# Three-stage kernel (causal attention, two expert layers): fixed places for early weight steps, a changed drain, and activations split by product

## The chip, the core and the metric

One core of one Trainium2 chip runs the whole program. The metric is the device time of one execution in microseconds, as the median of several runs. A profiled execution adds a trace: what each engine did and when, what ended its idle time, and the clock that TensorE was granted.

## The reference

Causal attention over 2 x 12 heads, 448 positions, 64 wide; then two feed-forward layers over the 896 rows of 768 columns, all in float32 accuracy (the weights come as 64-bit floats):

```python
scores = np.where(mask, -1e9, scale * q @ k.T)
attn = softmax(scores);  x = concat_heads(attn @ v)           # 896 x 768
h = x @ w_in                                                   # 768 x 2048
g = np.where(h >= 1, h, np.where(h <= -1, 0, (h + 1)**2 / 4))
x = g @ w_out                                                  # 2048 x 768
xn = x / rms(x) * rms_g
y = (silu(xn @ w_gate) * (xn @ w_val)) @ w_out2                # 768 x 1536, 1536 x 768
```

## The kernel before, in words

**Arithmetic.** A matrix operand is kept as two parts, a rounded high part and the rest, and a product of two such operands is three matmuls. `product` (L614) runs the three steps of 128 of half the inner size, so nine matmuls of 128x128 by 128x448. The w_in layer forms the output of a pair of column blocks for both batches with seven such products instead of eight (1 to 7, lines 723 to 770), out of sums and differences of blocks of the weights and of x. For the first four pairs products 1 and 2 are done early, as `head_in` and `tail_in` (L642, L646), so that five remain.

**Weights.** Each 128x768 block arrives by DMA into one of three stages (`w_load`, L141), always the next one in a fixed list `items`, and the load of a block waits until the block three places before it has left its stage (`w_next`, L149). The 64-bit words become float32 in steps: `w_scale` (GpSimd, L167, for the first NEARLY = 6 blocks, else ScalarE, L169), `w_low` (GpSimd, L177), `w_sign` (VectorE, L183, only where GpSimd scaled), `w_high` (VectorE, L195). Then the block is split (`parts`, L201: a cast on ScalarE, a subtraction on GpSimd), or, for a pair, first summed (`pair_steps` L416, `early_steps` L470: low, gate_high, val_high, sums_a, sums_b, hi, lo) and then split. A step is a small function; `steps` holds them in order, `ends` says where each block is finished, `w_run(n)` issues the next n up to a cap, `w_need(n)` issues all up to a block.

**Order.** Nothing is scheduled by a planner: each engine runs its instructions in the order in which the Python code issues them, so an instruction that waits holds all behind it on its engine. SP issues every DMA in the same way.

**Attention.** Twelve pairs of heads, three units each (L654). Per unit TensorE does scores, transposes of the exponentials and, once per pair, the spread of the factors (`spread`, L331) and the product with v (`pv`, L341); VectorE does the maxima (L277), ScalarE the exponentials (L285). One weight step is issued at the end of each unit from the second to the 35th (L701): first pairs 0 and 1 of the weights, then four plain blocks (the "gates") for the heads. When a pair's x is there, `xscale`, `xsplit` and `xmix` (L365 to L398) make the differences that the products need: T1 to T4, B11, B21, B22, each as high and low part.

**Drain.** Units 36 to 38 finish the last pair of heads. Heads and tails 0, 1, 2, 3 run there, two products to a unit, the product with v of the last pair between head 2 and tail 2 (L693 to L695); then its x is scaled, split and mixed.

**Layer with w_in.** For f = 0 to 7 a list `run` names the products in order (L792 to L799; pair f-1 still has 3 and 4 to do). After each product (L800):

```python
for p, g, n, late in run:
    IN[p][0](g)      # nine matmuls
    w_run(n)         # weight steps
    settle()         # clip of the product before
    IN[p][1](g)      # copy or sum, then relu and square
    w_run(late)
```

The activation is relu on ScalarE (L635), square on ScalarE (L637) or GpSimd (L639), and a clip on VectorE (L632) that `settle` issues later. Product 1 is copied out of its bank by ScalarE (L727) before product 6 adds into it; products 2, 4 and 5 are summed with earlier ones by VectorE (L718).

**w_out.** Sixteen blocks, three steps each, in a skewed order (L573): first step of block i, second of block i-1, third of block i-2. `out1` (L842) multiplies 18 matmuls per block. The second layer (from L961) follows the same plan as the first.

Of the kernel before, what the change touches and what calls it, by code (L numbers as in the profile page):

```python
# [41 lines left out]
def kernel(  # L42
# [14 lines left out]
    nc = tc.nc  # L57
# [16 lines left out]
    NEARLY = 6  # L74
# [290 lines left out]
    def xscale(g):  # L365
        b, p = divmod(g, NP)
        nc.vector.tensor_tensor(out=rb if b else X0[p], in0=xbank.pop(g)[:, :S], in1=rb, op=ALU.mult)

    def xsplit(g):
# [7 lines left out]
        else:  # L377
# [3 lines left out]
            if g == NG - 1:  # L381
                act_split(T2, k, t, nc.vector)
            else:
                pool_split(T2, k, t)
# [85 lines left out]
    def early_steps(n, f):  # L470
        bl = block(f)

# [12 lines left out]
        def gate_high():  # L485
            w_sign(n)
            w_high(n)
            w_low(n + 1)

        def val_high():  # L490
            w_sign(n + 1)
            w_high(n + 1)

        def sums_a():
            g, v, s12, s34 = halves(value(n)), halves(value(n + 1)), rest(n), rest(n + 1)
            tt(s12[:, 0], v[:, 0], v[:, 1], ALU.add)
            tt(s34[:, 0], g[:, 0], v[:, 0], ALU.subtract)

        def sums_b():
            g, s12, s34 = halves(value(n)), rest(n), rest(n + 1)  # L500
            tt(s12[:, 1], s12[:, 0], g[:, 0], ALU.subtract)
            tt(s34[:, 1], g[:, 1], s12[:, 1], ALU.subtract)
# [5 lines left out]
        def split_a():  # L508
            split(0, rest(n))
            w_next(n)  # L510

        def split_b():
            split(2, rest(n + 1))
# [5 lines left out]
        return [], [low, gate_high, val_high, sums_a, sums_b, split_a, split_b, split_c]  # L519
# [53 lines left out]
    def skewed(ws):  # L573
        for i in range(len(ws) + 2):
            for j in range(3):
# [5 lines left out]
    for w in work[:NW]:  # L581
        steps.extend(w)
        ends.append(len(steps))
    skewed(work[NW:NG2])
# [44 lines left out]
    def settle():  # L629
        while pending:  # L630
            out, u, x = pending.pop(0)
            nc.vector.scalar_tensor_tensor(out=out, in0=u, scalar=1.0, in1=x, op0=ALU.min, op1=ALU.max)  # L632

    def moe_act(out, u, x, eng=nc.scalar):
        nc.scalar.activation(u, x, ACTF.Relu, bias=half, scale=0.5)  # L635
        if eng is nc.scalar:
# [3 lines left out]
        pending.append((out, u, x))  # L640

    def head_in(f):  # L642
        product(bank(f), gop(f, 0), B11)
# [582 lines left out]
```

## Time and profile before

| | |
|---|---|
| median of 3 runs | 652.76 us (651.67 to 654.35) |
| the profiled execution, own time | 656.71 us |
| its span in the trace | 654.6 us |
| granted clock of TensorE, mean | 0.953 |
| busy: TensorE, VectorE, ScalarE, GpSimd | 597.6, 396.1, 349.5, 333.2 us |
| moved by DMA | 71.35 MB |

Busy time of TensorE counts matmuls at either clock level, so it is not time at full speed. An engine with time to spare can still hold up another one, if its instructions come in the wrong order; that is read from waits and timelines, not from busy shares.

### The profile page before, as it was taken

How to read it: one execution, taken by the hardware profiler on the slowest of the kernel's cores; microseconds unless marked ns; L12 is line 12 of the kernel's file. 1: busy time of each engine (PE TensorE's matmuls, PEld its weight loads, DVE VectorE, ACT ScalarE, POOL GpSimd, SP SyncE). 2: the span in 40 equal slices, each digit the busy share in tenths (PEclk: the TensorE clock that was granted, in tenths of full speed). 3: DMA queues.
4: the chain of work that ended last, by engine and by line, in shares of the span. 5: the costliest groups of instructions: out<-in, count | busy, mean ns of one | idle time of the engine just before them, and what ended most of it. 6: DMA issues, size and time to landing. Idle time of an engine off the chain costs nothing.

```text
span 654.6 us, 8698 instructions
## 1 busy us (share of the span) xinstructions
PE 597.6 (91%) x3164; PEld 508.7 (78%) x3164; DVE 396.1 (61%) x666; ACT 349.5 (53%) x698; POOL 333.2 (51%) x262
## 2 busy tenths in 40 slices
PE   6889999859959886589999999989999999999997
PEld 3556666748848785479889999979899999999996
DVE  4877888344664665347856684976565664896110
ACT  3767887435663555255476337755555555654211
POOL 3375656331675443349985543455555544894000
PEclk9897999878998888699999999998999999999999
DMA  8153533002332221245515320133353243551102
GB/s 285 44 182 119 183 105 126 1 1 97 96 105 88 97 96 48 103 164 208 201 49 193 102 91 8 42 117 124 105 173 109 98 132 114 189 192 47 39 0 86
DMA packets 17851, 71.35 MB, mean 109 GB/s; under 512 B 2128, under 2 KB 6736, under 8 KB 17808
## 3 DMA queue, kind: packets, MB, share of 16 engines
q1 hardware_dynamic: 17808, 70.79, 32.1%
q8 instruction: 25, 0.41, 0.2%
q14 instruction: 18, 0.15, 0.1%
HBM read 68.03 MB, written 2.75 MB: 108 GB/s over the span
## 4 chain that ended last, share of the span: by engine, by line
PE 71%; POOL 8%; ACT 7%; issue 5%; DVE 4%; DMA 4%; SPq 1%; POOLq 0%; DVEq 0%; ACTq 0%
PE ps L617 28%; PE ps L848 16%; PE ps L1160 14%; PE ps L270 4%; PE ps L301 4%; PE ps L349 4%; DMA af<-in_w_out 3%; POOL ar L203 2%; PE ps L335 2%; POOL af L177 1%; POOL af L639 1%; DVE af L355 1%; POOL ar L466 1%; ACT af L635 1%; ACT af L169 1%
## 5 line engine op out<-in xcount | busy, mean ns | idle before, releaser
L617 PE MATMUL ps<-ar 128*128 128x448 f32 x1260 | 277.9, 382 | 38.3 <-ACT af L727 14.5
L617 PEld LDWEIGHTS ps<-ar 128*128 128x128 f32 x1260 | 245.7, 197 | 68.4 <-ACT af L727 16.0
L203 POOL TENSOR_TENSOR ar<-af,ar 128x768 fp32r<-128x768 f32 (+1 forms) x56 | 101.2, 1809 | 97.9 <-ACT ar L202 85.8
L848 PE MATMUL ps<-ar 128*128 128x448 f32 x576 | 121.7, 372 | 2.5 <-POOL ar L203 1.8
L848 PEld LDWEIGHTS ps<-ar 128*128 128x128 f32 x576 | 109.0, 191 | 14.5 <-POOL ar L203 4.1
L177 POOL TENSOR_SCALAR af<-af 128x768 int32<-128x768 uint8 x76 | 83.4, 1097 | 23.2 <-DMA af<-in_w_out 17.3
L195 DVE SCALAR_TENSOR_TENSOR af<-af 128x768 int32<-128x768 int32 (+1 forms) x78 | 77.1, 992 | 24.1 <-POOL af L177 22.4
L1160 PE MATMUL ps<-ar 128*128 128x448 f32 x432 | 88.9, 367 | 0.0
L1160 PEld LDWEIGHTS ps<-ar 128*128 128x128 f32 x432 | 81.0, 188 | 7.7 <-DVE ar L1107 0.3
L169 ACT ACTIVATE af<-af 128x768 f32<-128x768 f32 x70 | 63.1, 909 | 44.0 <-DMA af<-in_w_out 44.0
L820 DVE TENSOR_TENSOR ar<-af,ar 128x448 fp32r<-128x448 f32 x32 | 46.5, 1471 | 23.6 <-ACT ar L819 23.6
L285 ACT ACTIVATE af<-ps,nm 112x336 f32<-112x336 f32 (+2 forms) x96 | 47.1, 504 | 22.9 <-DVE nm L277 22.8
L270 PE MATMUL ps<-af 64*112 64x448 f32 (+3 forms) x192 | 40.8, 476 | 10.5 <-DVE af L248 5.0
L202 ACT CAST ar<-af 128x768 fp32r<-128x768 f32 (+1 forms) x56 | 40.9, 731 | 17.5 <-DVE af L195 12.3
L632 DVE SCALAR_TENSOR_TENSOR af<-af,ps 128x448 f32<-128x448 f32 x24 | 14.9, 621 | 57.2 <-ACT af L637 40.2
L1107 DVE TENSOR_TENSOR ar<-af,ar 128x448 fp32r<-128x448 f32 x24 | 29.2, 1228 | 32.9 <-ACT ar L1106 32.8
L277 DVE CUSTOM_DVE_ANT_0 ps<-ps,af 112x336 f32<-112x336 f32 (+2 forms) x96 | 41.8, 469 | 8.4 <-PE ps L270 7.1
L466 POOL TENSOR_TENSOR ar<-af,ar 128x768 fp32r<-128x768 f32 x18 | 33.6, 1868 | 20.2 <-ACT ar L462 20.2
L270 PEld LDWEIGHTS ps<-af 64*112 64x112 f32 x192 | 18.7, 188 | 21.8 <-ACT af L285 6.2
L301 PE MATMUL ps<-ident,af 112*112 112x112 f32 x240 | 32.6, 278 | 2.0 <-ACT af L319 2.0
L635 ACT ACTIVATE af<-ps,half 128x448 f32<-128x448 f32 x24 | 15.2, 632 | 36.1 <-DVE ps L718 19.3
L941 POOL TENSOR_TENSOR ar<-af,ar 128x448 fp32r<-128x448 f32 x15 | 18.0, 1216 | 30.6 <-ACT ar L940 17.1
(101 smaller groups left out, 644.4 us busy)
## 6 DMA issues: line engine op xcount, KB each, us to landing
af<-in_w_out SPq DMA_DIRECT2D x28, 768.0 KB, 4.3
af<-in_w_in SPq DMA_DIRECT2D x20, 768.0 KB, 4.4
af<-in_w_gate SPq DMA_DIRECT2D x16, 768.0 KB, 4.4
af<-in_w_val SPq DMA_DIRECT2D x12, 768.0 KB, 4.3
af<-in_kT SPq DMA_DIRECT2D x12, 224.0 KB, 4.1
af<-in_qT SPq DMA_DIRECT2D x12, 224.0 KB, 4.3
af<-in_v SPq DMA_DIRECT2D x12, 224.0 KB, 2.8
out_T<-af SPq DMA_DIRECT2D x12, 224.0 KB, 1.9
```

The lines of the kernel that those rows point to most:

```text
L169: nc.scalar.activation(c, c, ACTF.Prelu, scale=2.0 ** -112, alpha=-2.0 ** 32)
L177: nc.gpsimd.tensor_scalar(out=words(n, 0, I32), in0=b, scalar1=1.0 / 32, scalar2=-31.0 / 64, op0=ALU.mult, op1=ALU.add)
L195: nc.vector.scalar_tensor_tensor(out=out.bitcast(I32), in0=words(n, 1, I32)[:, c], scalar=3, in1=words(n, 0, I32)[:, c], op0=ALU.logical_s ...
L203: nc.gpsimd.tensor_tensor(out=lo, in0=src, in1=b32(hi), op=ALU.subtract)
L270: nc.tensor.matmul(bs[j][:C, o:o + (c + 1) * C], lhsT=q[r, c * C:(c + 1) * C], rhs=k[r, :(c + 1) * C], start=True, stop=True, skip_group_c ...
L277: nc.vector.tensor_tensor_reduce(out=t, in0=t, in1=mask[:C, S - (c + 1) * C:], scale=-1.0, scalar=3e38, op0=ALU.add, op1=ALU.min, accum_ou ...
L285: nc.scalar.activation(Pn[:C, j, poff[c]:poff[c] + w], sbank[n][j][:C, o:o + w], ACTF.Exp, bias=nm[:C, j, c:c + 1], scale=-1.0, accum_out= ...
L301: nc.tensor.transpose(bs[j][:C, o:o + C], Pn[:C, j, poff[c] + kc * C:poff[c] + (kc + 1) * C], ident[:C, :C])
L617: nc.tensor.matmul(b[:, :S], lhsT=w(a, k), rhs=x[:, c, k], start=first and k == 0 and i == 0, stop=(k == HK - 1 and i == 2), skip_group_ch ...
L820: nc.vector.tensor_tensor(out=t[:, 1], in0=G[h][:, kk], in1=b32(t[:, 0]), op=ALU.subtract)
L848: nc.tensor.matmul(ybs[dm][:, :S], lhsT=w[:, a, dm * P:(dm + 1) * P], rhs=t[:, c], start=(n == 0 and i == 0), stop=(n == NM - 1 and i == 2))
L1160: nc.tensor.matmul(obs[dm][:, :S], lhsT=w[:, a, dm * P:(dm + 1) * P], rhs=t[:, c], start=(kk == 0 and i == 0), stop=(kk == NF - 1 and i == 2))
```

## The change

1. **Fixed table.** The gates come first in `items`, then the pairs. The steps of the gates and of pairs 0 and 1 are no longer in `steps`; a table `EARLY` names after which unit each of 37 steps is issued. NEARLY is 3. The steps of pair 0 and 1 are cut finer (eleven instead of eight).
2. **Second pair in the drain.** The last nine steps of pair 1 are placed at units 36 to 38. Its raw blocks and sums go to buffers that the attention has left by then.
3. **Product with v earlier.** Unit 36 runs only head 1, unit 37 the product with v and tail 1, unit 38 head 2, tail 2, head 3, tail 3.
4. **Last x in PSUM.** For the last pair of heads `xlast` takes the place of `xsplit` and `xmix`: x and the differences stay in PSUM banks, ScalarE casts, VectorE subtracts, in four pieces between the heads and tails.
5. **Activation split by product.** A sum or copy is issued right behind its product, then what `tick` finds due (relu and square at once, the clip one product later), then the weight steps. Some orders of products change (f = 1, f = 7).
6. **w_out steps.** The skewed order of the sixteen blocks runs back: third step of block i-2, second of i-1, first of i. The cap in f = 7 is one block lower.

The diff, cut (the finer cut of `early_steps`, names only changed, is left out):

```diff
-    NEARLY = 6
+    NEARLY = 3
...
     def xscale(g):
         b, p = divmod(g, NP)
-        nc.vector.tensor_tensor(out=rb if b else X0[p], in0=xbank.pop(g)[:, :S], in1=rb, op=ALU.mult)
+        x = xbank[g][:, :S] if g == NG - 1 else rb if b else X0[p]
+        nc.vector.tensor_tensor(out=x, in0=xbank[g][:, :S], in1=rb, op=ALU.mult)
...
+    def xlast():
+        g, k, p = NG - 1, HK - 1, NP - 1
+        x, t, x3, x4 = xbank[g][:, :S], bank(5)[:, :S], bank(6)[:, :S], bank(4)[:, :S]
+        sub(t, x, b32(T1[:, 0, k]))
+        sub(t, t, b32(T1[:, 1, k]))
+        yield
+        nc.scalar.copy(T2[:, 0, k], t)
+        sub(x3, t, X0[k])
+        sub(T2[:, 1, k], t, b32(T2[:, 0, k]))
+        yield
+        nc.scalar.copy(T3[:, 0, k], x3)
+        sub(x4, X0[p], t)
+        sub(T3[:, 1, k], x3, b32(T3[:, 0, k]))
+        yield
+        act_split(T4, k, x4, nc.vector)
+        act_split(B22, k, x, nc.vector)
+        yield
...
-        return [], [low, gate_high, val_high, sums_a, sums_b, split_a, split_b, split_c]
+        return [], [low, gate_high, val_low, val_high, sum_1, sum_3, sum_2, sum_4, split_a, split_b, split_c]
...
-    for f in range(2):
-        pair(f, True)
     for f in range(NA):
-        plain(w_in[PAIRS[f][0]], gslot(f), True)
-    for f in range(2, NPR):
+        plain(w_in[PAIRS[f][0]], gslot(f))
+    for f in range(NPR):
         pair(f, True)
...
-    def skewed(ws):
+    def skewed(ws, back=False):
         for i in range(len(ws) + 2):
-            for j in range(3):
+            for j in (2, 1, 0) if back else range(3):
...
-    skewed(work[NW:NG2])
+    skewed(work[NW:NG2], True)
...
+    EARLY = {(0, 2): ((0, 0), (0, 1), (1, 0)), (1, 2): ((0, 2),), (2, 0): ((0, 3),), (2, 2): ((1, 1),),
+             (3, 2): ((1, 2), (2, 0)), (4, 0): ((1, 3),), (4, 2): ((2, 1),), (5, 2): ((2, 2), (3, 0)),
+             (6, 0): ((2, 3),), (6, 2): ((3, 2), (4, 0)), (7, 0): ((3, 3),), (7, 2): ((4, 1), (4, 2)),
+             (8, 2): ((4, 3),), (9, 0): ((4, 4),), (9, 2): ((4, 5), (4, 6), (5, 0)), (10, 0): ((4, 7),),
+             (10, 2): ((4, 8),), (11, 0): ((4, 9),), (11, 1): ((4, 10),), (11, 2): ((5, 1),), (12, 0): ((5, 2),),
+             (12, 1): ((5, 3),), (12, 3): ((5, 4), (5, 5), (5, 6), (5, 7)), (12, 4): ((5, 8), (5, 9), (5, 10))}
...
             if g == NG:
-                head_in(2)
                 pv(g - 1)
-                tail_in(2)
+                tail_in(1)
         elif g == NG:
             xscale(g - 1)
-            xsplit(g - 1)
-            xmix(g - 1)
-        if 0 < n < NN - 1:
-            w_run(1)
-        if n in (NN - 1, NN, NN + 2):
-            f = n - NN + 1
-            w_need(4 + f + 1)
-            head_in(f)
-            tail_in(f)
+            mixing = xlast()
+            next(mixing)
+            head_in(2, lambda: next(mixing))
+            next(mixing)
+            tail_in(2)
+            settle()
+            next(mixing)
+            early(g, 3)
+            head_in(3)
+            tail_in(3)
+            early(g, 4)
+        early(g, u)
+        if n == NN - 1:
+            head_in(0)
+            tail_in(0)
+        elif n == NN:
+            head_in(1)
         settle()
...
         def in5(f):
-            x = gm(1, f, 1)
+            x, u = gm(1, f, 1), gm(1, f, 0)
             plus(x, yb[f], x)
             if 0 < f < NA - 1:
                 preload_in(f + 1)
-            moe_act(x, gm(1, f, 0), x, nc.gpsimd)
+            later(1, lambda: relu(u, x))
+            later(1, lambda: square(u, nc.gpsimd))
+            later(2, lambda: clip(x, u, x))
...
             if f == 0:
...
+                in6(0)
+                preload_in(1)
+                w_cap[0] = NA + 6
                 w_run(2)
-                in6(0)
-                settle()
-                preload_in(1)
...
-            w_cap[0] = 4 + NA + 2 * f if f < NPR - 1 else NW + 4
-            if f == 1:
-                run = [(6, 1, 2, 0), (3, 0, 1, 0), (7, 1, 0, 1), (4, 0, 1, 0), (5, 1, 0, 0)]
-            elif f < NA:
-                run = [(4, f - 1, 1, 0), (6, f, 1, 0), (3, f - 1, 2, 0), (7, f, 1, 1), (5, f, 1, 0)]
+            if f < NA:
+                run = [(4, f - 1, 1), (6, f, 1), (3, f - 1, 2), (7, f, 1), (5, f, 2)]
             elif f < NPR - 1:
-                run = [(p, f - (p in (3, 4)), 1, 0) for p in ((4, 1) if f == NA else (1, 4)) + (6, 3, 7, 5, 2)]
+                run = [(p, f - (p in (3, 4)), 1) for p in ((4, 1) if f == NA else (1, 4)) + (6, 3, 7, 5, 2)]
             else:
-                run = [(p, f - (p in (3, 4)), 2, 0) for p in (4, 3, 1, 6, 7, 2, 5)]
-                run[0] = (4, f - 1, 0, 0)
-            for p, g, n, late in run:
+                run = [(p, f - (p in (3, 4)), 1 + (p == 3)) for p in (4, 3, 1, 6, 7, 5, 2)]
+            for p, g, n in run:
                 IN[p][0](g)
+                IN[p][1](g)
+                tick()
                 w_run(n)
-                settle()
-                IN[p][1](g)
-                w_run(late)
```

The cap of the loop is now set ahead of it, to `NA + 2 * f + 4` for f < 7 and `NW + 3` for f = 7. Products 2, 3 and 4 are split as product 5 is; for 3 the relu follows at once. In the table (g, u) is the unit, the pair behind it a block (0 to 3 the gates, 4 and 5 the pairs) and one of its steps.

## Rows read from the trace of the kernel before

**Rows 1.** The page's head.

```profile
span 654.6 us, 8698 instructions
```

**Rows 2.** Busy time by stretch: PE, PEld, DVE, ACT, POOL, then granted clock.

```profile
0.00:64.00 64.00, 53.44 (x368) 33.28 (x368) 43.78 (x133) 39.62 (x124) 32.15 (x38) 0.89 0.47 159
...
115.00:148.60 33.60, 23.30 (x120) 18.80 (x121) 12.14 (x20) 12.70 (x26) 11.71 (x13) 0.85 0.00 1
148.60:275.00 126.40, 101.33 (x432) 88.70 (x433) 68.77 (x100) 64.72 (x104) 62.07 (x49) 0.88 0.27 89
```

**Rows 3.** The chain of waits in order of time: start, us, what.

```profile
19.32 0.92 PE ps L335 x16
...
62.47 0.92 PE ps L335 x16
...
70.32 0.92 PE ps L335 x16
...
255.64 4.18 DMA af<-in_w_out
...
459.19 103.05 PE ps L617 x504
```

**Rows 4.** VectorE's timeline: start, us, engine, line, tiles, idle before.

```profile
15.67 0.63 DVE L277 CUSTOM_DVE_ANT_0 ps<-ps,af 112x448 f32<-112x448 f32 x1
...
45.68 0.96 DVE L195 SCALAR_TENSOR_TENSOR af<-af 128x768 int32<-128x768 int32 x1 [0.79 <-POOL af L177]
...
126.62 0.20 DVE L328 RECIPROCAL rs<-rs 112x8 f32<-112x8 f32 x1
...
136.46 0.62 DVE L367 TENSOR_TENSOR af<-ps,af 128x448 f32<-128x448 f32 x1
...
156.33 0.62 DVE L718 TENSOR_TENSOR af<-ps,af 128x448 f32<-128x448 f32 x1 [5.98 <-PE ps L617]
...
208.50 2.24 DVE L632 SCALAR_TENSOR_TENSOR af<-af 128x448 f32<-128x448 f32 x1 [0.89 <-POOL af L639]
...
210.67 0.62 DVE L718 TENSOR_TENSOR ps<-ps,af 128x448 f32<-128x448 f32 x1
```

**Rows 5.** ScalarE's timeline.

```profile
211.38 0.63 ACT L635 ACTIVATE af<-ps,half 128x448 f32<-128x448 f32 x1 [3.92 <-DVE ps L718]
...
213.32 0.50 ACT L727 COPY af<-ps 128x448 f32<-128x448 f32 x1
```

**Rows 6.** TensorE's timeline.

```profile
130.47 2.11 PE L349 MATMUL ps<-af 112*64 112x336 f32 x20
...
143.07 3.64 PE L617 MATMUL ps<-ar 128*128 128x448 f32 x9 [6.65 <-ACT af L644]
...
148.62 21.65 PE L617 MATMUL ps<-ar 128*128 128x448 f32 x95 [1.92 <-ACT ps L721]
...
213.88 14.59 PE L617 MATMUL ps<-ar 128*128 128x448 f32 x63 [2.28 <-ACT af L727]
...
230.80 16.44 PE L617 MATMUL ps<-ar 128*128 128x448 f32 x72 [2.32 <-ACT af L727]
...
275.03 15.54 PE L848 MATMUL ps<-ar 128*128 128x448 f32 x72
...
293.74 53.68 PE L848 MATMUL ps<-ar 128*128 128x448 f32 x250 [1.80 <-POOL ar L203]
```

**Rows 7.** The page's costliest groups: count, busy us, mean ns, idle before.

```profile
L169 ACT ACTIVATE af<-af 128x768 f32<-128x768 f32 x70 | 63.1, 909 | 44.0 <-DMA af<-in_w_out 44.0
...
L466 POOL TENSOR_TENSOR ar<-af,ar 128x768 fp32r<-128x768 f32 x18 | 33.6, 1868 | 20.2 <-ACT ar L462 20.2
...
L462 ACT CAST ar<-af 128x768 fp32r<-128x768 f32 x18 | 15.1, 839 | 0.0
```

**Rows 8.** GpSimd's timeline in the w_out stage.

```profile
297.72 1.15 POOL L177 TENSOR_SCALAR af<-af 128x768 int32<-128x768 uint8 x1
...
301.66 1.15 POOL L177 TENSOR_SCALAR af<-af 128x768 int32<-128x768 uint8 x1
```

More of the change, by code (lines that the diff above doesn't have):

```diff
@@ L508, in split_a @@
         def split_a():
-            split(0, rest(n))
-            w_next(n)
+            split(0, operands()[2])
+            if not f:
+                w_next(n)
         def split_b():
-            split(2, rest(n + 1))
+            split(2, operands()[3])
         def split_c():
@@ L579, in skewed @@
                         ends.append(len(steps))
-    for w in work[:NW]:
-        steps.extend(w)
+    pre = work[:NA] + [work[NA + 1], work[NA + 3]]
+    for n, w in enumerate(work[:NW]):
+        if n >= NA + 4:
+            steps.extend(w)
         ends.append(len(steps))
-    skewed(work[NW:NG2])
+    skewed(work[NW:NG2], True)
     for n in range(NG2, W2_FIRST):
@@ L639, in moe_act, with clip, later, tick @@
             eng.tensor_tensor(out=u, in0=u, in1=u, op=ALU.mult)
-        pending.append((out, u, x))
-    def head_in(f):
+    def clip(out, u, x):
+        nc.vector.scalar_tensor_tensor(out=out, in0=u, scalar=1.0, in1=x, op0=ALU.min, op1=ALU.max)
+    def moe_act(out, u, x):
+        relu(u, x)
+        square(u)
+        pending.append(lambda: clip(out, u, x))
+    slots = []
+    def later(n, f):
+        slots.append([n, f])
+    def tick():
+        for x in slots:
+            x[0] -= 1
+        due = [x for x in slots if x[0] <= 0]
+        slots[:] = [x for x in slots if x[0] > 0]
+        for x in due:
+            x[1]()
+    def head_in(f, between=None):
         product(bank(f), gop(f, 0), B11)
+        if between:
+            between()
         nc.scalar.copy(first_in[f], bank(f)[:, :S])
@@ L754, in in2 @@
         def in2(f):
-            plus(cb, cb, gm(0, f, 0))
-            moe_act(gm(0, f, 0), gm(0, f, 0), cb)
+            u = gm(0, f, 0)
+            plus(cb, cb, u)
+            later(1, lambda: relu(u, cb))
+            later(1, lambda: square(u))
+            later(2, lambda: clip(u, u, cb))
         def p4(f):
@@ L761, in in4 @@
         def in4(f):
-            z = zb[f][:, :S]
-            plus(z, z, gm(0, f, 1))
-            moe_act(gm(0, f, 1), gm(0, f, 1), z)
+            z, u = zb[f][:, :S], gm(0, f, 1)
+            plus(z, z, u)
+            later(1, lambda: relu(u, z))
+            later(1, lambda: square(u))
+            later(2, lambda: clip(u, u, z))
         def p3(f):
@@ L769, in in3 @@
         def in3(f):
-            moe_act(gm(1, f, 0), gm(1, f, 0), yb[f][:, :S], nc.gpsimd)
+            y, u = yb[f][:, :S], gm(1, f, 0)
+            relu(u, y)
+            later(1, lambda: square(u, nc.gpsimd))
+            later(2, lambda: clip(u, u, y))
         IN = {1: (p1, in1), 2: (p2, in2), 3: (p3, in3), 4: (p4, in4), 5: (p5, in5), 6: (p6, in6), 7: (p7, in7)}
         for f in range(NPR):
+            w_need(NA + 2 * f + 2)
+            w_cap[0] = NA + 2 * f + 4 if f < NPR - 1 else NW + 3
             if f == 0:
                 preload_in(0)
-                w_cap[0] = 4 + NA + 2
                 p6(0, range(HK - 1))
@@ L833 @@
         presplit(2)
-        for p in (p4, p3):
-            p(NPR - 1)
+        for p in (4, 3):
+            IN[p][0](NPR - 1)
+            IN[p][1](NPR - 1)
+            tick()
             w_run(1)
-            settle()
-            (in4, in3)[p is p3](NPR - 1)
-        settle()
+        tick()
+        tick()
         w_cap[0] = NG2
```

42 lines of the change are left out of this document (26 added, 16 removed).

## The prediction, made before the changed kernel was run

> **What bounds the kernel now.** I began with the page: one execution spans 654.6 us [rows 1], and the kernel's own time for it is 656.71 us, so 2.1 us lie around the span. The median of the runs is 652.76 us, 3.95 below this execution. The sums are made against the execution, and the difference is then taken from the median.
>
> Next, the table by stretch, cut where the stages end: attention to 115 us, its drain to 148.6, the first expert layer's products to 275 [rows 2]. [...]
>
> The measure of a stretch without waits comes from the chain of waits [rows 3]. In the second layer 504 matmuls take 103.05 us: 204.5 ns each, 1.84 us for a product of nine. In the attention a pair of heads takes 7.85 us when dense (62.47 to 70.32), but the five pairs from 19.32 to 70.32 took 51.0 instead of 39.25: 11.75 lost. Near the end the chain runs through four transfers of w_out, the first from 255.64 and 4.18 us long.
>
> The engines' own timelines then say who waits. In the attention VectorE stands in a weight step for GpSimd (its step at 45.68 ends idle time on POOL's L177), and the maxima queued behind it come late [rows 4]. In the layer the order on VectorE is weight step, clip of the last product (which waits for GpSimd's square; 2.24 us at 208.50), then the sum of the product that has just ended, at 210.67 [rows 4]. ScalarE's relu waits 3.92 us for that sum, and the copy of product 1, which product 6 needs before it may add into the same bank, stands behind it at 213.32 [rows 5]. [...]
>
> **The change, part by part.**
>
> *Attention table.* The same eight blocks are prepared, gates first, 37 steps at fixed places instead of one per unit. GpSimd's part of a step stands one to three units ahead of VectorE's, so VectorE no longer waits in it. The loads follow their steps; blocks 0 to 2 are the same three transfers at the start, and the later ones are queued with q, k and v on SP, which are fetched three pairs ahead. This removes the 11.75 us. NEARLY 3 moves three scalings from GpSimd (and three sign steps from VectorE) to ScalarE: 3 x 0.91 = 2.7 us [rows 7], in a stage where ScalarE also does the exponentials. I let 0.75 of it reach the end: **-11.0**. Bounds: -13.5 (also the 1.7 us by which a step before them makes the maxima at 15.67 late [rows 4]) and -5 (the 2.7 us and one stall of 4 remain).
>
> *Drain, pv(11) moved ahead of two products.* It starts at 130.47 [rows 6]. Two products are 3.7 us, but the factors it follows are ready on VectorE only at 126.82 [rows 4], and their spread takes 0.92 [rows 3], so it moves by 2.7 and ends at 129.9. Its scaling still stands behind the clip of the product after it: 3.9 us, as 132.58 to 136.46 now [rows 4, 6]. So 133.8; two more VectorE steps of 0.62 and two ScalarE copies of 0.5 [rows 4, 5] put the first copy of head 2 at 136.8, while TensorE is done with tail 1 and head 2 at 133.6. After an idle of 6.65 us nine matmuls took 3.64 us (143.07) [rows 6], so I price tail 2 at that: 140.4. Head 3, its copy and tail 3 end at 145.3 (half of the first still slow), a relu of 0.63 and a square priced alike [rows 5], then pair 1's three casts, put into this queue by the table, 0.84 + 0.84 + 0.5 [rows 5, 7], and the preload 0.5: product 6 of pair 0 starts near 149.5 against 148.62. The differences kept in PSUM cost nothing themselves; every one is followed by a longer wait. [...]
>
> [...]
>
> *Activation split and step order in the layer.* A sum or copy now follows its product at once; relu and square come in the same tick, the clip one product later, and the weight steps after all of them. From the sum of product 5 of pair 0 (156.33) to the first w_out matmul (275.03) it is 118.7 us [rows 4, 6], holding 45 products: 82.8 at 1.84. The waits that I expect in the new order:
> - Pair 3: its casts and its low parts both come after the last product of f = 2. From that product's end: sum 0.62, preload and relu 1.1, cast 0.84, subtraction 0.6, in all 3.2 with the gaps, where product 6 wants it at 1.84: 1.4 us.
> - f = 4: product 6 comes straight after product 1, whose copy stands behind relu, square and two casts: 1.1 us. f = 7, the same neighbours with less in front: 0.65.
> - f = 5 and 6: product 2's sum, two casts, relu, square and product 1's copy end some 3.1 us after product 2; product 6 starts at 3.68. Nothing, but with 0.5 us to spare.
> - The clip of product 5 reads SBUF twice and may meet GpSimd's pair subtraction of 1.87 us [rows 7], as at 208.50. Queued behind it are the low part and so the next product 6: 0.4 per f, 2.8.
>
> That is 82.8 + 3.15 + 2.8 = 88.75: **-29.9**. Bounds: -33 (no clip is caught, pairs 3 and 4 in time) and -15 (next part). It includes the end of the chain: with the reversed skew the low step of one w_out block is queued before the first step of the block that waits for its transfer, so the fourth block's transfer is issued five products (9 us) and the fifth's three (5.5 us) before they are wanted, and the 4.2 us are hidden [rows 3]. The cap one block lower costs nothing: GpSimd has the third block done two us into the next stage, and it is read after 7.
>
> *First w_out products.* 275.03 to 293.74 held 74 matmuls, 15.1 us dense [rows 6]: 3.6 to gain. But GpSimd takes 3.94 us a block there (297.72 to 301.66) [rows 8] against 18 x 0.2045 = 3.68 on TensorE, and with thirteen blocks to go it ends at about 2 + 51.2, where the last two are wanted at 51.5 to 52.1: 1.1 back. **-2.5**, bounds -3.6 and 0.
>
> Sum: -11.0 + 1.0 - 29.9 - 2.5 = -42.4. The profiled execution would be 614.3, the median 652.76 - 42.4 = 610.4 us. From 400 us on nothing changes.
>
> **The rivals.**
> [...]
> - *The table only moves the attention's waits.* ScalarE is the fuller engine and has three scalings more; the exponentials come late instead of the maxima. The first part is then worth nothing: 621.
> - *The split does not do what it says*: product 6 still waits each time for a copy queued behind a relu, because the sum is late for another reason. Without the 29.9: 640.
> - *Slower.* Weight steps now stand behind the sum of the product just ended, so each slips by one product. If the seven steps of a pair, each waiting for the engine before, no longer fit into its loop, TensorE waits at the start of every f. [...] Against: GpSimd has under 9 us of work in a pair's 12.9.
>
> **How the numbers follow.** Forecast 0.62, pair loops 0.18, table 0.10, split without effect 0.05, slower 0.03; 0.02 that several fall short and it stays within 0.5%, which is about what a measurement of this kernel can tell from no change. The forecast's own bounds give 601 to 618; the loops with a poor table and a cold drain reach 632, so the range is 601 to 632, and what lies outside is the 0.10 of the last three cases and some of the tails. Faster 0.95, same 0.02, slower 0.03.
>
> **What would show it.** Right: pair distances of 7.9 us from the second pair on; VectorE's sum right behind each product; no TensorE wait over 1.5 us between product 6 of pair 0 and the w_out products, and a clock of 0.97 or more there; w_out transfers no longer in the chain. Wrong: waits on the copy of product 1 as long as now; the drain's product 6 later than 152 less the attention's 11; a clip of 2 us ahead of a pair's low part.

## The result, and the profile after

The changed kernel takes 630.96 us (median of 4 runs, 628.03 to 632.53), the kernel before 653.34 us beside it (4 runs): ratio 0.9655, 95% interval 0.9611 to 0.9698. It is faster by 22.4 us, where 42.4 were forecast, and the range of 601 to 632 just holds it. The profiled execution took 630.11 us, of which 628.4 are the span; that is 26.2 us shorter than the span of the profiled execution of before [rows 1].

The table by stretch is cut where the same stages end as in [rows 2]: attention, drain, the first layer's products, the w_out products, the rest. The columns are PE, PEld, DVE, ACT, POOL busy, then the granted clock.

```profile
0.00:101.00 101.00, 95.63 (x816) 62.31 (x816) 75.38 (x255) 81.77 (x255) 50.95 (x58) 1.00 0.44 145
101.00:135.80 34.80, 23.05 (x120) 18.71 (x121) 18.46 (x30) 15.93 (x33) 14.08 (x13) 0.90 0.13 46
135.80:240.00 104.20, 96.54 (x449) 86.29 (x450) 67.07 (x100) 64.11 (x105) 63.76 (x52) 0.97 0.34 114
240.00:375.00 135.00, 121.78 (x578) 107.92 (x577) 88.46 (x79) 65.97 (x103) 79.95 (x56) 0.97 0.38 129
375.00:628.40 253.40, 246.33 (x1204) 224.54 (x1203) 144.50 (x203) 124.32 (x208) 110.87 (x79) 0.99 0.30 102
```

In the first three stretches the clock is up, to 1.00, 0.90 and 0.97. TensorE idles for 5.4 us of 101 in the first and 7.7 of 104 in the third; in the drain it still idles for 11.8 of 34.8. New is the idle time of the fourth, the w_out stage: 13 us of 135. In the kernel before it was 2.5 of 125:

```profile
275.00:400.00 125.00, 122.45 (x592) 110.43 (x591) 83.46 (x81) 65.06 (x103) 85.12 (x54) 0.98 0.40 138
```

TensorE's timeline of the changed kernel shows where each stage begins and what it waits for:

```profile
17.37 0.99 PE L335 MATMUL ps<-ident,rs 112*64 112x112 f32 x16
25.68 0.99 PE L335 MATMUL ps<-ident,rs 112*64 112x112 f32 x16
...
57.10 0.99 PE L335 MATMUL ps<-ident,rs 112*64 112x112 f32 x16
...
102.76 2.07 PE L649 MATMUL ps<-ar 128*128 128x448 f32 x9
...
123.35 5.45 PE L649 MATMUL ps<-ar 128*128 128x448 f32 x18 [3.05 <-ACT af L699]
...
135.81 7.60 PE L649 MATMUL ps<-ar 128*128 128x448 f32 x27 [4.15 <-ACT ps L794]
...
180.93 41.95 PE L649 MATMUL ps<-ar 128*128 128x448 f32 x198 [3.52 <-ACT af L800]
224.00 11.21 PE L649 MATMUL ps<-ar 128*128 128x448 f32 x54 [1.13 <-ACT af L800]
235.06 0.36 PE L927 MATMUL ps<-ar 128*128 128x448 f32 x1
...
253.51 3.93 PE L927 MATMUL ps<-ar 128*128 128x448 f32 x18 [0.90 <-POOL ar L203]
258.35 3.92 PE L927 MATMUL ps<-ar 128*128 128x448 f32 x18 [0.90 <-POOL ar L203]
```

L335 opens a pair of heads, L649 is a product, L927 a w_out matmul. From such starts the difference of the two spans comes apart (after minus before, between the same events; all in us, from the two profiled executions):

| stretch | before | after | difference | forecast |
|---|---|---|---|---|
| start to first head | 116.67 | 102.76 | -13.9 | -11.0 |
| to product 6 of pair 0 | 31.95 | 33.05 | +1.1 | +1.0 |
| to first w_out matmul | 126.41 | 99.25 | -27.2 | -29.9 |
| to the next layer's first product | 125.28 | 139.75 | +14.5 | -2.5 |
| rest | 254.3 | 253.6 | -0.7 | 0 |

Three of the four terms are within 3 us of their forecasts. The fourth is 17 us off, and that is the miss. A w_out block of 18 matmuls, 3.9 us long, starts every 4.81 us (mean of the ten from 253.51 to 301.63), each time behind 0.90 us of waiting for GpSimd's low part (L203). Two blocks of the three other engines' timelines show that none of them is full either:

```profile
256.45 1.84 POOL L203 TENSOR_TENSOR ar<-af,ar 128x768 fp32r<-128x768 f32 x1 [1.76 <-ACT ar L202]
258.38 1.13 POOL L177 TENSOR_SCALAR af<-af 128x768 int32<-128x768 uint8 x1
261.26 1.83 POOL L203 TENSOR_TENSOR ar<-af,ar 128x768 fp32r<-128x768 f32 x1 [1.76 <-ACT ar L202]
...
256.87 1.90 DVE L898 TENSOR_TENSOR ar<-af,ar 128x448 fp32r<-128x448 f32 x1 [1.37 <-ACT ar L897]
258.70 1.61 DVE L195 SCALAR_TENSOR_TENSOR af<-af 128x768 int32<-128x768 int32 x1
...
255.53 0.84 ACT L202 CAST ar<-af 128x768 fp32r<-128x768 f32 x1 [1.66 <-DVE af L195]
256.27 0.56 ACT L897 CAST ar<-af 128x448 fp32r<-128x448 f32 x1
...
260.34 0.83 ACT L202 CAST ar<-af 128x768 fp32r<-128x768 f32 x1 [2.70 <-DVE af L195]
```

GpSimd is busy for 3.0 of 4.81 us and waits 1.76 for ScalarE's cast of the weights (L202). The cast waits 2.70 for VectorE's weight step (L195), and that stands behind VectorE's subtraction of an activation (L898). The subtraction waits for ScalarE's rounding of the same activation (L897), which stands behind the cast of the block before. It is a ring: cast, rounding, subtraction, weight step, next cast, from start to start 0.74 + 0.60 + 1.83 + 1.64 = 4.81 us. GpSimd's work hangs on the ring, and two links are long beside it: the subtraction takes 1.90 us while the low part runs (0.63 with no GpSimd work beside it, 258.36 in e2), and the weight step 1.61 while L177 does (0.96 where L177 has ended, 298.90 in the kernel before). In the kernel before, whose cast belonged to a block that the weight step had finished a round earlier, the same work took 3.94 us [rows 8].

### The profile page after: what moved, and what is told of

The parts are those of the page before. It is cut to its first block, busy times and chain, and to the rows that moved or that the text cites. A ratio compares the mean times of both kernels' runs of the same rounds, so it can differ in the third digit from the quotient of the medians.

```text
span 628.4 us, 8686 instructions
## 1 busy us (share of the span) xinstructions
PE 583.3 (93%) x3164; PEld 499.8 (80%) x3164; DVE 393.9 (63%) x665; ACT 352.1 (56%) x702; POOL 319.6 (51%) x256
## 4 chain that ended last, share of the span: by engine, by line
PE 75%; DVE 8%; ACT 7%; issue 6%; POOL 3%; DMA 0%; SPq 0%; DVEq 0%; POOLq 0%; ACTq 0%
PE ps L649 36%; PE ps L1239 14%; PE ps L927 11%; PE ps L270 5%; PE ps L301 4%; PE ps L349 3%; DVE af L195 3%; PE ps L335 1%; ACT ar L897 1%; ACT af L666 1%; ACT ar L202 1%; ACT af L285 1%; ACT af L169 1%; DVE af L355 1%; POOL af L177 1%
## 5 line engine op out<-in xcount | busy, mean ns | idle before, releaser
L649 PE MATMUL ps<-ar 128*128 128x448 f32 x1260 | 268.4, 374 | 18.5 <-ACT af L800 4.7
L649 PEld LDWEIGHTS ps<-ar 128*128 128x128 f32 x1260 | 239.6, 192 | 45.6 <-ACT af L699 5.6
L203 POOL TENSOR_TENSOR ar<-af,ar 128x768 fp32r<-128x768 f32 (+1 forms) x56 | 92.8, 1658 | 89.2 <-ACT ar L202 77.9
L927 PE MATMUL ps<-ar 128*128 128x448 f32 x576 | 124.2, 374 | 14.5 <-POOL ar L203 11.5
L927 PEld LDWEIGHTS ps<-ar 128*128 128x128 f32 x576 | 109.0, 191 | 28.9 <-POOL ar L203 16.5
L195 DVE SCALAR_TENSOR_TENSOR af<-af 128x768 int32<-128x768 int32 (+1 forms) x78 | 86.3, 1109 | 22.0 <-POOL af L177 12.6
L1239 PE MATMUL ps<-ar 128*128 128x448 f32 x432 | 87.9, 365 | 0.0
L1239 PEld LDWEIGHTS ps<-ar 128*128 128x128 f32 x432 | 81.1, 188 | 6.7 <-DVE ar L1186 0.3
L177 POOL TENSOR_SCALAR af<-af 128x768 int32<-128x768 uint8 x76 | 81.3, 1070 | 6.3
L169 ACT ACTIVATE af<-af 128x768 f32<-128x768 f32 x73 | 66.1, 912 | 11.9 <-DMA af<-in_w_out 11.9
L202 ACT CAST ar<-af 128x768 fp32r<-128x768 f32 (+1 forms) x56 | 41.0, 732 | 48.0 <-DVE af L195 42.9
L898 DVE TENSOR_TENSOR ar<-af,ar 128x448 fp32r<-128x448 f32 x32 | 43.2, 1363 | 37.7 <-ACT ar L897 37.7
L1186 DVE TENSOR_TENSOR ar<-af,ar 128x448 fp32r<-128x448 f32 x24 | 29.2, 1227 | 32.3 <-ACT ar L1185 32.3
L270 PE MATMUL ps<-af 64*112 64x448 f32 (+3 forms) x192 | 37.6, 462 | 4.7 <-DVE af L248 4.5
L1020 POOL TENSOR_TENSOR ar<-af,ar 128x448 fp32r<-128x448 f32 x15 | 18.0, 1214 | 30.5 <-ACT ar L1019 17.1
L672 POOL TENSOR_TENSOR af<-af 128x448 f32<-128x448 f32 x16 | 16.0, 1001 | 32.3 <-ACT af L666 30.1
L301 PEld LDWEIGHTS ps<-ident,af 112*112 112x112 f32 x240 | 23.9, 138 | 9.7 <-issue 4.2
L358 POOL TENSOR_SCALAR ar<-af 128x448 fp32r<-128x448 f32 x15 | 9.6, 639 | 38.2 <-DVE rs L327 38.2
```

The lines of the kernel that those rows point to most:

```text
L169: nc.scalar.activation(c, c, ACTF.Prelu, scale=2.0 ** -112, alpha=-2.0 ** 32)
L177: nc.gpsimd.tensor_scalar(out=words(n, 0, I32), in0=b, scalar1=1.0 / 32, scalar2=-31.0 / 64, op0=ALU.mult, op1=ALU.add)
L195: nc.vector.scalar_tensor_tensor(out=out.bitcast(I32), in0=words(n, 1, I32)[:, c], scalar=3, in1=words(n, 0, I32)[:, c], op0=ALU.logical_s ...
L202: nc.scalar.copy(hi, src)
L203: nc.gpsimd.tensor_tensor(out=lo, in0=src, in1=b32(hi), op=ALU.subtract)
L270: nc.tensor.matmul(bs[j][:C, o:o + (c + 1) * C], lhsT=q[r, c * C:(c + 1) * C], rhs=k[r, :(c + 1) * C], start=True, stop=True, skip_group_c ...
```

## The experiments

Each ran beside the kernel before on the same chip, but e1 to e4, e5 to e8, e9 to e11 and e12 on four different ones. The kernel before had medians of 653.3 to 655.6 us in these groups, so between groups a difference of two or three microseconds says little. "Layer" is product 6 of pair 0 to the first w_out matmul, "w_out" the stage behind it, both from the one profiled execution of each kernel (us; "about" where the first start lies inside a merged row).

| kernel | median us | ratio to before, 95% | layer | w_out |
|---|---|---|---|---|
| changed | 630.96 | 0.9655 (0.9611 to 0.9698) | 99.3 | 139.8 |
| e1 order of w_out steps back | 637.49 | 0.9737 (0.9716 to 0.9758) | 102.1 | 143.4 |
| e2 reversed for 7 rounds only | 621.18 | 0.9485 (0.9462 to 0.9509) | 100.3 | 131.1 |
| e3 activation split out of PSUM | 614.94 | 0.9398 (0.9374 to 0.9422) | 100.3 | 124.5 |
| e4 preload first | 624.50 | 0.9549 (0.9524 to 0.9575) | about 99 | 138.7 |
| e5 = e3 + e4 | 610.95 | 0.9354 (0.9326 to 0.9382) | about 99 | 125.9 |
| e6 weight steps first | 633.60 | 0.9700 (0.9664 to 0.9736) | 104.9 | 138.1 |
| e7 before, w_out steps reversed | 654.40 | 1.0026 (0.9997 to 1.0055) | 117.1 | 133.8 |
| e8 = e7, split out of PSUM | 637.92 | 0.9774 (0.9740 to 0.9808) | 118.7 | 121.2 |
| e9 = e5, copy of head 2 first | 605.58 | 0.9255 (0.9221 to 0.9289) | about 99 | 124.4 |
| e10 scalings back on GpSimd | 632.21 | 0.9643 (0.9597 to 0.9690) | 100.3 | 140.1 |
| e11 clip at once | 648.04 | 0.9882 (0.9835 to 0.9929) | 119.6 | 138.7 |
| e12 = e9, low part later | 605.51 | 0.9266 (0.9234 to 0.9298) | about 98 | 124.4 |

**e1, the old order of the w_out steps.**

```diff
-    skewed(work[NW:NG2], True)
+    skewed(work[NW:NG2])
```

> The changed kernel with only the order of the w_out steps put back: in each round low part of block k+2, first step of block k+1, second half of block k. Theory A (the reversed order makes each block's subtraction follow a cast of the same round, and VectorE's subtractions stand behind GpSimd's; this costs 0.87 us a block, 4.81 us against 3.94): the rounds come back to 3.9 to 4.0 us and the stage of the w_out products, 139.9 us in the changed kernel, shrinks to 124 to 127; in exchange the transfers of the fourth to sixth block are again issued late and the first w_out matmul comes 8 to 15 us later than 235.06. Sum: 624 to 632, about the changed kernel's 631. Rival B (the longer rounds come from something else, the clock or the contraction buffers): rounds stay at 4.8, and the late transfers come on top: 640 to 646. Rival C (the late transfers were never what the first product waited for): rounds 3.94 and no later start: 614 to 617.

It came out worse than every number of A: 637.5. The first w_out matmul is only 2.6 us later (237.68), but the chain of waits (start, us, what) now runs through one transfer after another, seven from 231 to 290 us, six of them inside the stage; these are the first three:

```profile
231.07 4.02 DMA af<-in_w_out
...
243.42 4.10 DMA af<-in_w_out
...
252.66 4.39 DMA af<-in_w_out
```

So the reversed order does what its step in the prediction said, and its price in this kernel is less than what it saves. The rounds between two transfers do fall below 4 us, but no steady 3.94 appears; from the old order alone the ring can't be judged.

**e2, reversed for seven rounds, then the old order.**

```diff
-            for j in (2, 1, 0) if back else range(3):
+            for j in (2, 1, 0) if i < back else range(3):
...
-    skewed(work[NW:NG2], True)
+    skewed(work[NW:NG2], 7)
```

> The changed kernel with the reversed order kept for the first seven rounds of w_out steps, where it hides the transfers, and the order of before from there on. Theory A: first w_out matmul at 235 as in the changed kernel, rounds of 3.9 to 4.0 us after it, the stage 125 to 129 us instead of 139.9, no wait of TensorE of 0.9 us a block on the low part: 616 to 621. Rival B (the depth of the order is not the cause): rounds stay at 4.8 and the time at 629 to 633.

621.2 is 0.2 us above A's range. The first matmul stays at 235.9, the 0.9 us a block go, and 8.7 of the lost 14.5 us come back. The rest is again the transfers: ScalarE's scaling (L169) idles 18.6 us for them in 256 to 300 us.

**e3, the activation split out of PSUM.** The order is untouched; only where VectorE's subtraction reads one of its operands is changed.

```diff
-            nc.scalar.copy(t[:, 0], G[h][:, kk])
-            nc.vector.tensor_tensor(out=t[:, 1], in0=G[h][:, kk], in1=b32(t[:, 0]), op=ALU.subtract)
+            src = G[h][:, kk]
+            if g == 0 and j >= 4:
+                src = bk(6 + j % 2)[:, :S]
+                nc.scalar.copy(src, G[h][:, kk])
+            nc.scalar.copy(t[:, 0], src)
+            nc.vector.tensor_tensor(out=t[:, 1], in0=src, in1=b32(t[:, 0]), op=ALU.subtract)
```

> The changed kernel in which, for blocks 4 to 15 of the first half of the w_out products, ScalarE first copies the activation into a free PSUM bank, and its cast and VectorE's subtraction read it there. It adds twelve ScalarE copies of about 0.5 us, off the path, and leaves the order of the steps. Theory A, second half (VectorE's subtraction takes 1.9 us instead of 0.6 because it reads two SBUF operands while GpSimd does): the group of that subtraction falls to 0.6 to 0.7 us a block, the first step of the next block starts up to 1.2 us earlier, and the round falls from 4.81 to between 3.9 and 4.3: 619 to 627. Rival D (only the dependence counts: the cast follows the first step of the same round, and that step is held by GpSimd alone): the subtraction gets short, the round stays at 4.7 to 4.8, 629 to 633. Rival E (the subtraction is long for a reason of its own): it stays at 1.9 us and so does the time.

614.9 is 4 us below A's range, so the gain is larger than A said, and D and E are out. The groups of 256 to 300 us (count, busy us, mean ns, idle before), first of the changed kernel:

```profile
L203 POOL TENSOR_TENSOR ar<-af,ar 128x768 fp32r<-128x768 f32 x10 | 18.3, 1832 | 17.5 <-ACT ar L202 17.5
L898 DVE TENSOR_TENSOR ar<-af,ar 128x448 fp32r<-128x448 f32 x9 | 17.1, 1895 | 12.3 <-ACT ar L897 12.3
L195 DVE SCALAR_TENSOR_TENSOR af<-af 128x768 int32<-128x768 int32 x9 | 14.6, 1622 | 0.0
```

and of this kernel, where the subtraction is L902 and the added copy L900:

```profile
L203 POOL TENSOR_TENSOR ar<-af,ar 128x768 fp32r<-128x768 f32 x11 | 20.4, 1854 | 4.2 <-ACT ar L202 4.2
...
L195 DVE SCALAR_TENSOR_TENSOR af<-af 128x768 int32<-128x768 int32 x10 | 11.8, 1183 | 0.0
...
L902 DVE TENSOR_TENSOR ar<-ps,ar 128x448 fp32r<-128x448 f32 x10 | 6.2, 625 | 19.7 <-ACT ar L901 19.7
...
L900 ACT COPY ps<-af 128x448 f32<-128x448 f32 x10 | 5.3, 529 | 0.0
```

The subtraction falls from 1895 to 625 ns, the weight step behind it from 1622 to 1183, and GpSimd's idle time from 17.5 to 4.2 us. TensorE then runs nine blocks without a gap:

```profile
258.14 33.31 PE L931 MATMUL ps<-ar 128*128 128x448 f32 x163 [0.27 <-POOL ar L203]
```

That is 204.4 ns a matmul, the dense pace of [rows 3]. The subtraction still runs while a low part does, so it is the place of its operand and not the moment that makes it short:

```profile
263.48 1.86 POOL L203 TENSOR_TENSOR ar<-af,ar 128x768 fp32r<-128x768 f32 x1 [0.20 <-ACT ar L202]
...
264.43 0.62 DVE L902 TENSOR_TENSOR ar<-ps,ar 128x448 fp32r<-128x448 f32 x1 [1.90 <-ACT ar L901]
```

So the reversed order made the ring (e2 and e7), and VectorE's two long instructions beside GpSimd's made it too long. The ring is still there, with the added copy as a fifth link, but it takes 3.62 us from cast to cast (262.56 to 266.18), just under TensorE's 3.68 a block. Beside the same low part the subtraction is 1.90 us with two SBUF operands and 0.62 with one.

**e4, the preload of pair 0 first.**

```diff
             head_in(3)
+            nc.scalar.copy(bank(0)[:, :S], first_in[0])
             tail_in(3)
             early(g, 4)
...
-                preload_in(0)
```

> The changed kernel with the preload of pair 0's bank issued on ScalarE right behind the copy of head 3, ahead of the relu and square of tail 3 and of the three casts of pair 1 that the table puts there. Theory F (the 4.15 us that TensorE waits ahead of product 6 of pair 0 are a matter of ScalarE's order alone): the wait falls to under 0.6 us, product 6 starts at 131 to 132 instead of 135.81, and because pair 1's casts are 0.5 us later at most nothing else moves: 626 to 628 (0.5 to 0.7% below the changed kernel). Rival G (the early start only moves the wait: pair 0's products 6 and 7, or pair 1's, stand for GpSimd's halves of the blocks, which come no sooner): TensorE waits 3 to 4 us within the next ten products and the time stays at 630 to 632.

F holds: tail 3 starts 0.79 us behind head 3, product 6 follows it in one row, and the drain falls from 33.05 to about 28.6 us. 624.5 is 6.5 below the changed kernel, more than the wait of 4.15 and 1.5 below F's range; G is out.

```profile
129.33 7.96 PE L649 MATMUL ps<-ar 128*128 128x448 f32 x36 [0.79 <-ACT af L699]
```

**e5, both.** The two diffs above together.

> Both edits that shortened the changed kernel, together: the activation of blocks 4 to 15 split out of PSUM, and the preload of pair 0's bank ahead of tail 3's relu and pair 1's casts. Alone they gave 16.0 and 6.5 us (614.9 and 624.5 against 631.0). They lie in different stages (240 to 303 us, and 131 to 136). If the two losses are independent, the sum holds: 607 to 610. If the earlier layer only makes the w_out weights late (the w_out stage is then bound by its transfers), part comes back: 612 to 615.

611.0, 1 us above the range for independent losses and 2.5 above the plain sum. The next layer begins at 356.78, 4.3 us earlier than in e3, where e4 alone gave 5.9. In the two profiled executions the missing part is clock: behind the same wait of 1.22 us the next 67 matmuls took 13.84 us in e3, at a granted clock of 1.00, and 15.61 here, at 0.89.

```profile
288.54 15.61 PE L931 MATMUL ps<-ar 128*128 128x448 f32 x67 [1.22 <-POOL ar L203]
```

**e6 and e11, the two halves of the activation split undone one at a time.** e6:

```diff
                 IN[p][0](g)
+                w_run(n)
                 IN[p][1](g)
                 tick()
-                w_run(n)
```

> The changed kernel with one part of the new order undone: the weight steps of a product stand again ahead of its sum and its relu and square, as in the kernel before (the later clip stays). [...] Rival I (the order of the steps is worth nothing; the gain of the stretch came from the clip moved a product later and from the transfers of w_out): distances stay at 12.8 to 13.3 and the time at 629 to 634.

e11, in all four places:

```diff
-            later(2, lambda: clip(x, u, x))
+            later(1, lambda: clip(x, u, x))
```

> The changed kernel with the other half of the activation split undone: the clip of a product is issued in the same tick as its relu and square, not one product later. The stretch from product 6 of pair 0 to the first w_out matmul is 99.25 us in the changed kernel and 126.41 in the one before; the reversed order alone gave 9.3 of that, putting the weight steps first takes back 5.6. Theory R (what is left, 12.3 us, is the clip's delay, since a clip waits on VectorE for a square and holds the sum of the next product and with it the copy of product 1): the stretch comes to 107 to 113 us, TensorE waits 1.5 to 4 us ahead of a product 6 in most pairs, and the time is 638 to 645. Rival S (the sum right behind its product does it all, wherever the clip stands): the stretch stays under 102 us and the time at 629 to 634.

e6 is 2.6 us slower by the medians, with intervals that overlap, so I holds in the time. In the distances it does not: VectorE's sums of product 5 of pairs 4 to 6 come 14.1 to 14.2 us apart, where I said 13.3 at most and the changed kernel has 12.76.

```profile
204.48 0.62 DVE L791 TENSOR_TENSOR af<-ps,af 128x448 f32<-128x448 f32 x1
...
218.65 0.62 DVE L791 TENSOR_TENSOR af<-ps,af 128x448 f32<-128x448 f32 x1
```

TensorE itself waits only 0.20 us in pairs 5 and 6. The sums fall behind it, and the lag is paid ahead of product 6 of pair 7, with a wait of 3.77 us where the changed kernel has 1.13. The layer is 5.6 us longer and the w_out stage 1.7 shorter. e11 loses 17.1 us by the medians, 14.8 by the ratios, and its layer of 119.6 is beyond R's 113. Its TensorE waits again in almost every pair, and VectorE shows why: a clip that waits for GpSimd's square stands ahead of the next sum.

```profile
156.88 9.38 PE L649 MATMUL ps<-ar 128*128 128x448 f32 x45 [2.61 <-ACT af L812]
...
241.22 12.49 PE L649 MATMUL ps<-ar 128*128 128x448 f32 x54 [4.53 <-ACT af L800]
```

```profile
185.45 0.62 DVE L675 SCALAR_TENSOR_TENSOR af<-af 128x448 f32<-128x448 f32 x1 [1.75 <-POOL af L672]
...
186.86 0.62 DVE L791 TENSOR_TENSOR ps<-ps,af 128x448 f32<-128x448 f32 x1
```

With e7, which has neither half (and is otherwise the kernel before), the layer takes 99.3 us with both, 104.9 with the late clip alone, 119.6 with the early sum alone and 117.1 with neither. The late clip is the gain; the early sum is worth something only beside it.

**e7 and e8, the reversed order on the kernel before**, without and with the split out of PSUM (the edit of e3):

```diff
-            for j in range(3):
+            for j in (2, 1, 0) if back else range(3):
...
-    skewed(work[NW:NG2])
+    skewed(work[NW:NG2], True)
```

> The kernel before with the reversed order of the w_out steps and nothing else of the change. Theory A: the four serial transfers ahead of the first w_out matmul are hidden, which brings it 8 to 12 us forward of 275.03; the rounds behind it then take 4.8 us instead of 3.94 and give back 10 to 13. So the two halves of this part cancel: 650 to 658, against 654.5 of the kernel before here. Rival J (the transfers were hidden anyway, or something else ends as late): no gain in front, the loss behind: 662 to 668. Rival K (the longer rounds need the rest of the change): gain without loss: 641 to 646.

> The kernel before with the reversed order of the w_out steps and the activation split of blocks 4 to 15 read out of PSUM. Theory A: first w_out matmul 8 to 12 us forward of 275.03 and rounds of 3.6 to 3.7 us, set by TensorE, in place of 3.94: 638 to 645, that is 10 to 16 below the kernel before. Rival J (nothing gained in front): 649 to 653. Rival L (the reading out of PSUM helps only where ScalarE has the room that the changed order of the layer leaves it): rounds above 4.2 and 645 to 652.

A holds both times, e8 a little below its lower end of 638. e7 gains 9.3 us in the layer, where the transfers were, and gives 8.5 back in the w_out stage: no difference that can be measured. The round of 4.81 us is there without the rest of the change:

```profile
299.57 3.91 PE L848 MATMUL ps<-ar 128*128 128x448 f32 x18 [0.90 <-DVE ar L820]
304.39 3.90 PE L848 MATMUL ps<-ar 128*128 128x448 f32 x18 [0.91 <-DVE ar L820]
```

e8 turns that into 15.8 us of gain, with 323 w_out matmuls in one row, 3.75 us a block of 18, a little over the 3.7 said:

```profile
267.59 67.30 PE L852 MATMUL ps<-ar 128*128 128x448 f32 x323 [0.57 <-DVE ar L824]
```

**e9, the copy of head 2 ahead of the first cast of the last x.**

```diff
         product(bank(f), gop(f, 0), B11)
+        nc.scalar.copy(first_in[f], bank(f)[:, :S])
         if between:
             between()
-        nc.scalar.copy(first_in[f], bank(f)[:, :S])
```

> The shortened kernel (activation split out of PSUM, preload ahead) with one more edit in the drain: ScalarE's copy of head 2 is issued ahead of the first cast of the last x, where the changed kernel has it behind. In the changed kernel that copy stands at 122.76 behind a cast that waits 2.56 us for VectorE, and TensorE waits 3.05 us for it ahead of tail 2. Theory M (the wait is ScalarE's order alone): tail 2 follows head 2 within 0.7 us, the drain from the first head to product 6 of pair 0, 29.3 us in the shortened kernel (103.09 to 132.3), falls to 25 to 27, and the time from 610.95 to 606 to 609. Rival N (product 6 of pair 0 waits for the last x, whose two differences come out of VectorE's queue no sooner): TensorE stands ahead of product 6 or 7 of pair 0 instead, and the time stays at 610 to 613.

M holds in the wait and the drain, with a time just below its 606. Tail 2 follows head 2 after 0.62 us, tail 3 still waits 1.74, the drain is about 25.7 us, and 605.6 is 25.4 us below the changed kernel, 0.9255 of the kernel before.

```profile
121.09 3.91 PE L649 MATMUL ps<-ar 128*128 128x448 f32 x18 [0.62 <-ACT af L697]
126.74 7.94 PE L649 MATMUL ps<-ar 128*128 128x448 f32 x36 [1.74 <-ACT af L697]
```

**e10, three blocks' scalings back on GpSimd.** The table has no place for the sign step of block 3, so this kernel leaves that one step of VectorE out.

```diff
-    NEARLY = 3
+    NEARLY = 6
...
         def gate_high():
+            w_sign(n)
...
         def val_high():
+            w_sign(n + 1)
             w_high(n + 1)
```

> The changed kernel with the scalings of three more blocks put back on GpSimd, and their sign steps back on VectorE, as in the kernel before; the fixed table stays. The first part measured 13.9 us (first head matmul at 116.67 and 102.76) where 11.0 was forecast, 0.75 of it a charge for these scalings on ScalarE. Theory O (on ScalarE they are hidden, and so they are on GpSimd): first head matmul at 102.3 to 103.3 and the time at 629 to 633. Theory P (on ScalarE they cost their 0.75): 0.5 to 1 us earlier and 629 to 631. Theory Q (that they left GpSimd and VectorE is a part of the 13.9): first head matmul 1.5 to 4 us later, 632 to 636.

O holds: the first head starts at 103.00 against 102.76, the time is 632.2. As far as a run without that step can tell, where the scalings stand costs nothing in this table.

**e12, pair 4's low part behind the sum.**

```diff
-            w_need(NA + 2 * f + 2)
+            if f != NA:
+                w_need(NA + 2 * f + 2)
...
-                run = [..., (5, f, 2)]
+                run = [..., (5, f, 1 + (f < NA - 1))]
...
-                run = [(p, f - (p in (3, 4)), 1) for p in ...]
+                run = [(p, f - (p in (3, 4)), 1 + (f == NA and p == 4)) for p in ...]
```

> The shortest kernel so far (activation split out of PSUM, preload ahead, copy of head 2 ahead) with the last step of pair 4, its low parts, moved from behind product 5 of pair 3 to behind the sum of product 4. In the changed kernel TensorE waits 3.52 us ahead of product 6 of pair 4, where 1.1 was forecast: VectorE's sum of product 4 starts at 177.70, 2.3 us after its product, because that low part, issued ahead of it, waits until 176.83 for ScalarE's cast; the relu, the square and the copy of product 1 follow the sum. Theory T (the step in front of the sum makes the wait): the wait falls to 1.2 to 2.2 us, then set by the low part itself, which product 6 reads, behind product 5's clip, and the time from 605.6 to 602.5 to 604.5. Rival U (product 6 would stand for its own low parts as long, now that a clip of 1.7 to 2.3 us is ahead of them): the wait stays over 3 us and the time at 605 to 607.

Neither T nor U. The sum comes at once (168.15, 0.6 us behind the one before it), but ScalarE's relu now stands behind the two casts of the pair, so the wait falls from 3.53 to 2.51 us only, and the time does not differ from e9's.

```profile
172.71 41.95 PE L649 MATMUL ps<-ar 128*128 128x448 f32 x198 [2.51 <-ACT af L801]
```

## Why the prediction was right in sign and 20 us off in size

**Attention: the mechanism right, the term 2.9 too small.** From the second pair on the distance is 7.85 us (25.68 to 57.10 are four of them), as it would show if right; only the last three, from 72.82 on, are 7.93 to 8.34. VectorE's three waits for GpSimd's L177 are gone from 14 to 64 us, and TensorE's 5.4 us of waits there with them. Two sizes were off. The first pair's 1.9 us (19.25 to 17.37) stood in the bound and not in the term. And the 0.75 charged for the scalings on ScalarE were not there (e10). The table itself was not undone on the chip, so that it removed these waits is read from the timelines.

**Drain: right, by its own steps.** Forecast an idle of 3.2 us ahead of tail 2, measured 3.05; product 6 was put 0.9 us later than before (149.5 against 148.62), which is the +1.0 of the sum, measured 1.1. The cold drain in the range was not shown: tail 2 took 3.62 us for its nine matmuls, as priced, but head 3 behind it 1.83, at a granted clock of 1.00. The match of the idle time is partly luck: the product with v took 3.73 us (112.73) where 2.1 were said, and where it takes 2.09, as in e3, the idle time is 4.08. The working's 136.8 also needs the scaling's own 0.62 us, which it does not name: the terms named come to 136.0. What the prediction took as given, ScalarE's order, was the larger price: e4 and e9 take 7.3 us off the drain by moving two copies.

**Layer: right in mechanism and nearly in size.** Pairs 5 and 6 run without a wait, 12.76 us apart on VectorE's sums, where seven products at 1.84 and 0.4 for the clip make 13.3. The hidden transfers are worth 9.3 of the 27.2 on the kernel before (e7), the split and its order the rest, most of it the late clip (e6, e11); taken back out of the changed kernel they cost only 2.8 there (e1), so the parts do not simply add up. Off was the wait for f = 4: 3.52 us, where 1.1 was said and nothing over 1.5 was to show. The prediction counted what stands ahead of product 1's copy on ScalarE and left out that VectorE's sum of product 4 is itself held, by a low part that waits for a cast:

```profile
176.83 0.96 DVE L447 TENSOR_TENSOR ar<-ps,ar 128x768 fp32r<-128x768 f32 x1 [1.43 <-ACT ar L477]
177.70 0.62 DVE L791 TENSOR_TENSOR ps<-ps,af 128x448 f32<-128x448 f32 x1
```

That is not all of it. With the low part out of the way (e12) the wait is still 2.51 us, so 1.4 of the 2.4 missed belong to ScalarE's relu behind the two casts, which the prediction named and counted too short.

**First w_out products: the step that failed.** "GpSimd takes 3.94 us a block there" carried the old round over to the new order. The reversed skew was followed for what it hides, the transfer, and not for what it makes dependent: block k's cast now follows block k's weight step in the same round. And the 3.94 us were no pace of GpSimd's own: its low part, 2.62 us there (295.02, behind the start of VectorE's weight step at 294.97), takes 1.84 in the changed kernel (256.45), where it starts ahead of VectorE's subtraction. The prediction weighed this wait for the clip of product 5, at 0.4 us a pair, and not for the thirteen blocks where both engines work without pause. With the subtraction's operand in PSUM the term is -0.8 (e3) to -4.1 (e8), on either side of the -2.5 forecast, and the whole kernel is at 614.9 us against 610.4 forecast; but that is another kernel than the one that was predicted.

**The rivals.** Pair loops at the 16.9 us of before (213.88 to 230.80 [rows 6]): no, 12.76. The table only moves the waits: no. Split without effect, and slower: no. No rival had a w_out stage longer than before. That the range holds 630.96 is luck too: its upper end, 632, was made of slow pair loops, a poor table and a cold drain, none of which came, and its bound for the w_out term was 0, not +14.5. The misses of the attention (2.9 us better) and the layer (2.7 worse) cancel.

## What to carry to other kernels

When the order of a software pipeline is reversed, follow each stage's operands for one round anew: an order that issues a load earlier may make two stages of the same block meet in one round, and the old round time says nothing of the new one. Where VectorE and GpSimd work side by side, an operand of VectorE in PSUM, for a ScalarE copy of 0.53 us a block, was worth 16 us here. An operation that waits for another engine belongs behind, not ahead of, what the bound engine needs next; the late clip was the larger half of what the activation split gained.

## What the runs showed of the hardware

- VectorE and GpSimd each had long instructions beside the other's. In the kernel before, GpSimd's low part at 298.95 takes 2.63 us, with VectorE's weight step under way from 298.90 (0.96 us), and VectorE's subtraction at 299.78 takes 2.28, with the low part under way. The low part takes 1.84 where it starts first (256.45 in the changed kernel), and the subtraction 0.63 where no GpSimd work meets it (the last row, of e2).

```profile
298.90 0.96 DVE L195 SCALAR_TENSOR_TENSOR af<-af 128x768 int32<-128x768 int32 x1 [0.78 <-POOL af L177]
299.78 2.28 DVE L820 TENSOR_TENSOR ar<-af,ar 128x448 fp32r<-128x448 f32 x1
...
298.95 2.63 POOL L203 TENSOR_TENSOR ar<-af,ar 128x768 fp32r<-128x768 f32 x1
...
258.36 0.63 DVE L898 TENSOR_TENSOR ar<-af,ar 128x448 fp32r<-128x448 f32 x1 [2.19 <-ACT ar L897]
```

- An operand in PSUM made VectorE's subtraction no slower: 625 ns as the mean of ten in e3, against 0.63 us for one with two SBUF operands that met no GpSimd work (258.36 in e2, above).
- Behind the same short wait the granted clock differed: 1.22 us, then 67 matmuls in 13.84 us in one kernel (e3, granted clock 1.00) and 15.61 in another (e5, 0.89). A difference of 2 us between the profiled executions of two kernels is therefore no finding here.
